# An attention-and-MLP kernel on one core: all products in 32-column shape, zero-padded queries for single score banks, and merges done by accumulating transfers

## The chip, the cores and the metric

The kernel runs on one core of a Trainium2 chip. The metric is the device time of one execution in microseconds (us); less is better. Engines are named as in the profile: PE is TensorE (PEld its weight loads), ACT is ScalarE, DVE is VectorE, POOL is GpSimd, and SP is SyncE, which here only issues transfers.

## The reference

For one sequence of 2048 rows and 448 columns, with 16 heads of 28 columns and a hidden width of 1792 (all data in bf16):

```python
xn = layernorm(A_x)
q, k, v = heads(xn @ A_wqkv)                       # 16 heads, 28 columns each
p = softmax(q @ k.T * 28 ** -0.5)                  # 2048 x 2048 scores for each head
s = merge_heads(p @ v) @ A_wo
g = silu(gelu(xn @ B_w1 + B_b1) @ B_w2 + B_b2)     # tanh form of GELU
out = A_x + s * g
```

`B_x` is not used. The exponentials are the large part: 16 x 2048 x 2048 of them.

## The kernel before

**Tiles.** Each head is padded to 32 rows, so that four heads (a group, G = 4 of them) fill the 128 partitions. Queries are cut into C = 4 chunks of 512 and keys into T = 16 tiles of 128. A block is one group with one query chunk; there are 16 blocks, each of 64 score banks (16 key tiles x 4 heads), 1024 in all. A score bank holds 128 keys x 512 queries in one of seven PSUM banks called `ring`; the eighth bank, `acc`, holds the attention output of the current block. The last block is cut into three parts by query, so that the end of the kernel can start early.

**Scores** (L1617) contract over 32 rows, so they use a strip of 32 rows of PE; four of them with different strips run at once. **Attention products** (L2052) put 32 output rows (28 values, one sum, padding) into one strip of 32 columns of PE; four of them run at once too. All other products use the full 128 x 128 array: query and key projections (L1042), value projections (L1390), the first MLP layer (L1468), the second (L1537), the output projection (L2140), and a product with zeros that only keeps PE busy (L1227). Some projections do the last 32-row pieces of their contraction together with scores (L1058, L1423, L1438). So PE changes between three shapes.

**Exponentials.** ACT takes two or three neighbouring score banks in one instruction (L1671) and writes bf16 tiles. Some banks ("late" ones, four at a time, the heads of one key tile) go to DVE instead: L1901 turns the score into the bits of a bf16 by a multiply and an add to uint16, and L1960 makes two shifted copies of the four banks (2048 values a row) by integer adds, so that the sum of the three approximates the exponential better. The three copies are multiplied by the values, the two shifted ones by values scaled by 0.6875 (`vs`, L1985), which takes 12 attention products a late group. A **merge** adds the two shifted copies first, which leaves 8 products. Before, POOL does it in four additions of 512 columns (L1973).

**The end of a block.** `acc` is copied to SBUF (L2111); its four rows of sums go to DRAM (L2117) and come back spread over 128 partitions (L2119), POOL raises them to the power -1 (L2121), they go out again (L2123) and come back repeated over the rows (L2126), and POOL multiplies (L2130). The output projection of a query chunk needs all four groups. Between GM = 582 and the next units, ACT changes its table and does all GELUs at once, partly straight out of PSUM (L1515).

**Order.** A scheduler runs at build time: generators (`p_scores`, `p_exps`, `p_pv`, `p_late`, `p_f1` and others) offer tasks with an estimated duration, and `run` picks for each engine the task that can start first, within `EPS`, by priority. A row of tuned constants per block (`BP`) steers it. On a change of PE's shape it adds `SWITCH` = 0.1 us, and `rate` prefers tasks of the shape that PE is in. What comes out is one fixed list per engine. Engines wait for each other by semaphores, and each works strictly through its own list. `p_solo` and `attach` place late scores: in strips of rows that a pair of scores leaves free, or alone.

Of the kernel before, what the change touches and what calls it, by code (L numbers as in the profile page):

```python
# [16 lines left out]
DH = 28  # L17
# [13 lines left out]
BPN = ('S4', 'QF', 'MG', 'GQ', 'GE', 'EPS', 'HP', 'JIT', 'RM', 'RG', 'WT', 'PV0', 'PVC', 'MP', 'ND4', 'LU', 'JOINT', 'LQ', 'JMAX', 'DQ', 'URG', 'SLACK', 'UR', 'QLEAD', 'QDIST', 'R3')  # L31
BP = (
# [17 lines left out]
)  # L50
NQ = (14, 15, 11, 13, 12, 16, 14, 5, 16, 15, 16, 16, 16, 16, 14, 16)
# [10 lines left out]
MG, GQ, GE = 1, 4.0, 12  # L62
GP, MP4, GL = 4.64, 1, 1.2
# [25 lines left out]
SEM, OWN = 0.07, 0.03  # L89
# [5 lines left out]
EA = 1  # L95
G3P = 0
# [15 lines left out]

class _Task:
    __slots__ = ("E", "fn", "reads", "writes", "dur", "lat", "rank", "w", "mode", "rows", "port")
# [5 lines left out]
    def __init__(self, E, fn, reads=(), writes=(), dur=0.1, lat=0.05, prio=5, w=1.0, mode="full", rows=(), port=False):  # L120
        self.E, self.fn, self.reads, self.writes = E, fn, list(reads), list(writes)
        self.dur, self.lat, self.rank, self.w = dur, lat, prio, w
        self.mode, self.rows, self.port = mode, set(rows), port
        if E == DVE:
            ov = min(OVERLAP, 0.4 * self.dur)
            self.dur, self.lat = self.dur - ov, self.lat + ov


class _Kernel:
# [55 lines left out]
    def start_of(self, t):  # L185
# [14 lines left out]
        for b in t.writes:  # L200
            mine = b.w is not None and b.w[0] is own
            if not (t.E == PE and mine):
                s = max(s, (b.tw or 0.0) + (OWN if mine else SEM))
            s = max(s, b.tr + SEM)
        return s

    def put(self, t, start=None):
# [3 lines left out]
        sem = self.evsem[t.E]  # L211
        self.evcnt[t.E] += 1
# [6 lines left out]
        self.prog[t.E].append(lambda eng, f=t.fn, s=sem: f(eng).then_inc(s, 1))  # L219
        h = (sem, self.evcnt[t.E])  # L220
# [276 lines left out]
    def alloc(self):  # L497
# [16 lines left out]
        self.P = sb("P", [128, NP, 512], bf)  # L514
        self.E_sb = sb("E_sb", [128, 2, 512], bf)
# [94 lines left out]
        self.b_dum = B()  # L610
        self.b_vs = [[B() for _ in range(NS)] for _ in range(2)]
# [27 lines left out]
        self.s_x0b, self.s_wqk1 = self.sem("s_x0b"), self.sem("s_wqk1")  # L639
        self.s_out = [self.sem("s_out%d" % q) for q in range(14)]  # L640
        self.s_w = {n: self.sem("s_" + n) for n in ("wqk", "wv", "w1", "w2", "wo", "b")}

    def schedule(self):
# [41 lines left out]
        K.a_left = {}  # L685
        K.h3_free = False
# [328 lines left out]
    def t_tr(self, c, pr, h, bank, tok, prio=5):  # L1015
# [11 lines left out]
        return _Task(PE, f, K.b_xn[c % 3][2 * h:2 * h + 2] + [K.b_id], [tok], 0.225, 0.17, prio)  # L1027
# [71 lines left out]
    def p_first(self):  # L1099
# [32 lines left out]
        def tr(pr, h):  # L1132
# [10 lines left out]
            return _Task(PE, f, K.b_xn[0][2 * h:2 * h + 2] + [K.b_id], [tok], 0.225, 0.17, 0)  # L1143
# [11 lines left out]
        def proj(which, h, k, bank, tok):  # L1155
# [8 lines left out]
            return _Task(PE, f, [K.b_wqk[which][0], K.b_pads, K.b_xnT[0][k] if h else K.b_x0h[k]], [tok], 0.218, 0.17, which)  # L1164
# [24 lines left out]
    def p_q0(self, h, bank, tok):  # L1189
# [5 lines left out]
                                               skip_group_check=True), [K.b_qsq[h], K.b_bsel], [tok], 0.11, 0.17, 0)  # L1195
# [7 lines left out]
    def p_warm(self, cond):  # L1203
# [4 lines left out]
        while cond():  # L1208
            yield _Task(PE, lambda eng: eng.matmul(bank[:, 0:256], K.ident[:, :], K.E_sb[:, 0, 0:256], start=True, stop=True),
                        [K.b_id, K.b_pads], [tok], 0.22, 0.1, 95)  # L1210
# [9 lines left out]
    def p_busy(self):  # L1220
# [3 lines left out]
        def f(eng):  # L1224
            ins = None
            for _ in range(3):
                ins = eng.matmul(K.acc[:, 0:128], K.zero[:, :], K.ident[:, :], start=False, stop=True,  # L1227
                                 skip_group_check=True)
# [9 lines left out]
    def p_norm(self, g0, g1, pr=1):  # L1238
        K = self
        bank, tok = yield ("bank", lambda: True, pr)  # L1240
# [9 lines left out]
        yield _Task(PE, f, K.b_wsq[g0:g1] + [K.b_pads], [tok], 0.15 * n + 0.1, 0.1, pr, 0.15)  # L1250
# [27 lines left out]
    def p_tr(self, c, pr):  # L1278
        K = self
        bank, tok = yield ("bank", lambda: K.ln_done >= 2 * (c + 1) and K.ready(K.b_xn[c % 3], 0.5), 1.5)  # L1280
# [49 lines left out]
    def p_q(self, g, c):  # L1330
# [21 lines left out]
        yield _Task(PE, lambda eng: eng.matmul(bank2, K.bsel[:, :], qs, start=True, stop=True),  # L1352
# [27 lines left out]
    def t_v(self, ts, h0, h1, bank, tok, ks=range(KT)):  # L1380
# [3 lines left out]
        def f(eng):  # L1384
            ins = None
            for i, t in enumerate(ts):
                off = i * nh * DH
                for kt in ks:
                    ap = bass.AP(tensor=K.wv, offset=kt * WS + h0 * DH, ap=[[KT * WS, 128], [1, nh * DH]])
                    ins = eng.matmul(bank[:, off:off + nh * DH], K.xnT[:, kt, t * 128:(t + 1) * 128], ap,  # L1390
                                     start=(kt == 0), stop=(kt > 0), skip_group_check=True)
# [71 lines left out]
    def t_f1(self, c, ft, bank, tok, k, prio=None):  # L1463
# [3 lines left out]
        def f(eng):  # L1467
            return eng.matmul(bank, K.w1[:, k, ft * 128:(ft + 1) * 128], K.xnT[:, k, c * 512:(c + 1) * 512],  # L1468
                              start=(k == 0), stop=(k > 0), skip_group_check=True)
# [19 lines left out]
    def p_gelu(self):  # L1489
# [4 lines left out]
        for q, pc in enumerate(PIECES):  # L1494
# [16 lines left out]
            for f in range(f0, f0 + n):  # L1511
# [4 lines left out]
                        wr, 0.4267 * n + (0.1 if pc else 0.06) + (1.3 if q == 0 else 0), 0.05, -1)  # L1516
# [4 lines left out]
        K.tE[ACT] += 1.3  # L1521
# [5 lines left out]
    def p_f2(self, c, t):  # L1527
# [5 lines left out]
        for q in range(7):  # L1533
            def f(eng, q=q):
                ins = None
                for ft in (2 * q, 2 * q + 1):
                    ins = eng.matmul(ps, hv[:, ft, t * 128:(t + 1) * 128], K.w2[:, ft, :],  # L1537
                                     start=(ft == 0), stop=(ft == FT - 1))
# [205 lines left out]
    def unit_of(self, b, n=1):  # L1744
# [21 lines left out]
    def p_late(self):  # L1766
        K = self
        yield ("until", lambda: K.late_on)
        K.spawn(K.p_room(), 0)
        K.spawn(K.p_solo(), 0, lambda: len(K.lq) > 0 and K.urgent(K.lq[0][0]))  # L1770
# [29 lines left out]
    def p_solo(self):  # L1800
        K = self
        while True:
# [3 lines left out]
            now = lambda: len(K.lq) > 0 and K.can(K.lq[0][0], K.now) and (K.in_gelu() or K.next_m >= MTOT or K.urgent(K.lq[0][0]))  # L1806
# [13 lines left out]
            for (m0, u, m), x in rs:  # L1820
                K.spawn(K.p_apass(u, m0, m - m0, *x), m0)

# [121 lines left out]
    def p_expq(self, m0, u):  # L1944
# [7 lines left out]
        for _ in range(2):  # L1952
            v = K.unit_of(b)
# [9 lines left out]
        if MG and K.next_m < 64 * (m0 // 64 + 1) - GE and K.tE[POOL] < K.now + GQ:  # L1963
            v, w = us[1:]
            for k in range(0, 4, MP4):
                if MP4 > 1:
                    W, X = K.pair(v, w)
                else:
                    W, X = K.part(v, k), K.part(w, k)
                    if len(W.shape) != len(X.shape):  # L1970
                        W, X = (x if len(x.shape) == 3 else x.rearrange("p (a b) -> p a b", b=128) for x in (W, X))
                bs = K.b_U[v][k:k + MP4], K.b_U[w][k:k + MP4]
# [271 lines left out]
```

## Time and profile before

| | |
|---|---|
| median of 3 runs | 426.02 us (424.85 to 426.95) |
| span of the profiled execution, first to last instruction | 425.0 us |
| PE busy, instructions | 403.8 us, 3705 products |
| ACT busy | 407.8 us, 435 instructions |
| DVE busy | 345.9 us, 588 instructions |
| POOL busy | 214.2 us, 214 instructions |
| exponentials on ACT (L1671) | 346 of two banks, 32 of three |
| exponentials on DVE (L1901) | 236 banks |
| merges on POOL (L1973) | 64 additions for 16 merges |

The profiled execution is given by its span alone; the median of the timed runs lies 1.0 us above it. Instructions of PE and ACT overlap their neighbours, so a length in the profile is longer than the step from one start to the next, and a busy share near 100% does not tell by itself which engine is the limit.

### The profile page before, as it was taken

The page shows a single profiled execution, that of the slowest core. Times are in us where ns is not written, and L with a number is a line of the kernel's source. Part 1 is how long each engine was busy: PE and PEld are TensorE (multiplying, and loading weights), DVE is VectorE, ACT ScalarE, POOL GpSimd, SP SyncE. Part 2 cuts the span into 40 slices and gives each one's busy share as a digit, 9 for nine tenths or more (in the row PEclk, how much of TensorE's full clock was granted, in tenths as well). Part 3 has the DMA queues.
Part 4 walks back from the last instruction along what each step waited for, and adds up shares of the span by engine and source line. Part 5 has one row for each costly group of instructions (what it writes and reads, how often), then busy time and mean ns, then how long its engine had stood idle before and what let it go on. Part 6 is the DMA issues. An engine that isn't in the chain of part 4 may idle for free.

```text
span 425.0 us, 9807 instructions
## 1 busy us (share of the span) xinstructions
PE 403.8 (95%) x3705; PEld 134.1 (32%) x3705; DVE 345.9 (81%) x588; ACT 407.8 (96%) x435; POOL 214.2 (50%) x214
## 2 busy tenths in 40 slices
PE   6999999999999999999999999999999999999985
PEld 4533222333222222222223442332222233223452
DVE  8969998579989998999975127679789968899865
ACT  6999999999999999999999999999999999999983
POOL 7590330784291405406374324677599678523720
PEclk9999999999999999999999999999999999999998
DMA  8702000010000000100230100001000010206232
GB/s 259 267 3 39 2 27 2 2 26 17 27 1 27 2 25 4 29 2 2 59 122 27 26 0 2 2 3 26 2 3 25 3 28 2 69 3 113 25 73 66
DMA packets 17721, 15.31 MB, mean 36 GB/s; under 512 B 8893, under 2 KB 14761, under 8 KB 17642
## 3 DMA queue, kind: packets, MB, share of 16 engines
q1 hardware_dynamic: 16810, 13.07, 11.3%
q0 software_dynamic: 576, 0.92, 1.7%
q8 instruction: 30, 0.49, 0.5%
q10 hardware_dynamic: 288, 0.69, 0.4%
q14 instruction: 17, 0.14, 0.1%
HBM read 12.60 MB, written 2.94 MB: 37 GB/s over the span
## 4 chain that ended last, share of the span: by engine, by line
PE 66%; DVE 14%; ACT 13%; issue 5%; POOL 1%; POOLq 0%; DVEq 0%; ACTq 0%
PE ring L1617 17%; PE acc L2052 15%; PE ring L1468 9%; PE ring L1537 9%; ACT P L1671 9%; PE ring L1042 5%; ACT h L1671 3%; DVE w L1901 3%; PE ring L2140 2%; PE ring L1438 2%; PE ring L1390 2%; DVE x_sb L1960 2%; PE ring L1058 2%; DVE h L1960 1%; DVE h L1450 1%
## 5 line engine op out<-in xcount | busy, mean ns | idle before, releaser
L1671 ACT ACTIVATE P<-ring 128x1024 bf16<-128x1024 f32 (+1 forms) x262 | 259.2, 1114 | 1.5 <-PE ring L1617 1.1
L1617 PE MATMUL ring<-qT,kT 32*128 32x512 bf16 (+2 forms) x1152 | 148.6, 359 | 6.3 <-ACT P L1671 1.7
L1671 ACT ACTIVATE h<-ring 128x1024 bf16<-128x1024 f32 (+1 forms) x82 | 86.0, 1139 | 2.0 <-PE ring L1617 1.8
L1617 PEld LDWEIGHTS ring<-qT,kT 32*128 32x128 bf16 x1152 | 40.1, 91 | 121.3 <-ACT P L1671 59.8
L2121 POOL TENSOR_TENSOR rc<-rs,mone 128x16 f32<-128x16 bf16 x15 | 46.6, 3104 | 21.5 <-DMA rs<-sums 21.4
L1537 PE MATMUL ring<-w,h 128*128 128x448 bf16 x224 | 55.0, 356 | 0.6 <-ACT xnT L1671 0.5
L1468 PE MATMUL ring<-xnT,w 128*128 128x512 bf16 x201 | 54.3, 382 | 0.8 <-DVE w L1901 0.6
L2052 PE MATMUL acc<-P,vaug 128*32 128x512 bf16 (+2 forms) x627 | 52.8, 354 | 0.0
L1901 DVE TENSOR_SCALAR x_sb<-ring 128x512 uint16<-128x512 f32 x64 | 42.8, 685 | 8.4 <-PE ring L1617 8.0
L1671 ACT ACTIVATE xnT<-ring 128x1024 bf16<-128x1024 f32 (+1 forms) x34 | 35.4, 1119 | 1.6 <-PE ring L1617 1.6
L1901 DVE TENSOR_SCALAR w<-ring 128x512 uint16<-128x512 f32 x52 | 34.4, 684 | 1.0 <-PE ring L1617 0.7
L1901 DVE TENSOR_SCALAR h<-ring 128x512 uint16<-128x512 f32 x40 | 27.0, 686 | 3.7 <-PE ring L1617 3.2
L2130 POOL TENSOR_TENSOR qT<-x_sb,E_sb 128x512 bf16<-128x512 f32 x15 | 18.1, 1209 | 22.8 <-DMA x_sb<-recs 22.6
L1345 POOL TENSOR_TENSOR qsq<-qT 128x512 bf16<-128x512 bf16 x12 | 12.7, 1071 | 32.7 <-DVE qT L1339 31.4
L1468 PEld LDWEIGHTS ring<-xnT,w 128*128 128x128 bf16 x201 | 16.5, 97 | 28.0 <-issue 9.4
L2052 PE MATMUL acc<-h,vaug 128*32 128x512 bf16 x213 | 24.7, 385 | 0.3 <-DVE w L1960 0.2
L1537 PEld LDWEIGHTS ring<-w,h 128*128 128x128 bf16 x224 | 16.1, 97 | 25.8 <-issue 15.5
L1339 DVE CAST qT<-ring 128x512 bf16<-128x512 f32 x15 | 10.3, 686 | 13.2 <-PE ring L1042 13.1
L1985 POOL TENSOR_SCALAR vs<-vaug 128x128 bf16<-128x128 bf16 x32 | 10.2, 320 | 21.0 <-PE acc L2052 10.7
L2052 PEld LDWEIGHTS acc<-P,vaug 128*32 128x32 bf16 x627 | 13.9, 95 | 16.7 <-issue 13.7
L2140 PE MATMUL ring<-wo,qT 128*128 128x448 bf16 x64 | 17.0, 386 | 2.3 <-POOL qT L2130 1.5
L1450 DVE TENSOR_SCALAR h<-ring,b1c 128x512 bf16<-128x512 f32 x23 | 17.0, 744 | 2.4 <-PE ring L1438 1.2
(232 smaller groups left out, 657.0 us busy)
## 6 DMA issues: line engine op xcount, KB each, us to landing
x_sb<-recs SPq DMA_DIRECT2D x60, 64.0 KB, 2.0
w<-in_B_w_dram SPq DMA_DIRECT2D x1, 1568.0 KB, 7.7
w<-in_B_w_dram SPq DMA_DIRECT2D x1, 1344.0 KB, 8.5
x_sb<-in_A_x_dram SPq DMA_DIRECT2D x2, 448.0 KB, 5.6
out_dram<-in_A_x_dram SPq DMA_DIRECT2D x2, 448.0 KB, 10.0
out_dram<-h POOLq DMA_DIRECT2D x4, 224.0 KB, 4.3
out_dram<-h SPq DMA_DIRECT2D x8, 112.0 KB, 1.7
h<-in_A_wqkv_dram SPq DMA_DIRECT2D x3, 168.0 KB, 5.2
```

Of the source, the lines that this page charges most:

```text
L1042: return eng.matmul(bank, w[:, k, g * 128:(g + 1) * 128], K.xnT[:, k, c * 512:(c + 1) * 512], start=(k == 0), stop=(k > 0), skip_group_che ...
L1450: yield _Task(DVE, lambda eng: eng.tensor_scalar(dst, bank, K.b1c[:, ft:ft + 1], None, op0=ALU.add), [tok, K.b_b1c], wr, 0.69, 0.0, 2)
L1468: return eng.matmul(bank, K.w1[:, k, ft * 128:(ft + 1) * 128], K.xnT[:, k, c * 512:(c + 1) * 512], start=(k == 0), stop=(k > 0), skip_grou ...
L1537: ins = eng.matmul(ps, hv[:, ft, t * 128:(t + 1) * 128], K.w2[:, ft, :], start=(ft == 0), stop=(ft == FT - 1))
L1617: return eng.matmul(dst, K.kT[32 * j:32 * j + 32, g, t * 128:(t + 1) * 128], K.qT[32 * j:32 * j + 32, g, c * 512 + q0:c * 512 + q0 + nq], ...
L1671: return eng.activation(reg[:, i0:i0 + n, :], src, ACTF.Exp, scale=SM_SCALE)
L1901: yield _Task(DVE, lambda eng: eng.tensor_scalar(K.part(u, k).bitcast(dt.uint16), K.like(u, bank), SM_SCALE * LOG2E * 128.0, (127.0 - EXP_ ...
L1960: yield _Task(DVE, lambda eng, W=W, T=T, i=i: eng.tensor_scalar(W.bitcast(u16), T.bitcast(u16), float(SH[i]), None, op0=ALU.add), bT, bW, ...
L2052: return eng.matmul(K.acc[32 * j:32 * j + 32, q0:q0 + nq], w, ap[:, col:col + nq] if len(ap.shape) == 2 else ap[:, col // 128:(col + nq) / ...
L2121: yield _Task(POOL, lambda eng: eng.tensor_tensor(K.rc[:, :], K.rs[:, :], K.mone[:, 0:1].to_broadcast([128, 16]), ALU.pow), [K.b_srs, K.b_ ...
L2130: yield _Task(POOL, lambda eng: eng.tensor_tensor(dst, K.rb, E, ALU.mult), [K.b_rb, tE], [K.b_onT[g][c]], 1.15, 0.05, 1, port=True)
L2140: ins = eng.matmul(ps, K.qT[:, g, c * 512 + t * 128:c * 512 + (t + 1) * 128], K.wo[:, g, :], start=(g == 0), stop=(g == G - 1))
```

## The change

Full-array products become four products of 32 columns each (`_mm`), which run beside each other in the four column strips. They are then of the same shape as the attention products, so that `mode` now knows mostly rows and columns; only transposes, the norm products and the start keep the full array. For each block the queries of the fourth head are copied into a buffer whose other rows are zero (`qpad`); a late score of that head can then be computed over all 128 rows, in column shape, in a bank of its own (`p_alone`). The merge becomes one transfer on POOL's queue from SBUF to SBUF which adds to its destination (512 KB, eight semaphores in turn); there are 41 of them. From the twelfth block on (`RV` = 11, blocks 11 to 14) the reciprocal of the sums is taken by DVE and not by POOL. The constants per block, the number of late groups that may be taken (`NQ`) and some estimated durations differ, and with them the order on every engine. Late banks are 244 instead of 236.

```diff
-NQ = (14, 15, 11, 13, 12, 16, 14, 5, 16, 15, 16, 16, 16, 16, 14, 16)
+NQ = (14, 6, 16, 11, 11, 16, 14, 3, 9, 15, 16, 16, 5, 13, 5, 12)
...
+TXI, TXL = 0.95, 5.0
+CN, CS, SR = 1, 3.0, 1
+PJ = 3
...
+RV = 11
...
+def _mm(eng, out, w, x, start, stop):
+    ins = None
+    for q in range(0, 128, 32):
+        ins = eng.matmul(out[q:q + 32, :], w[:, q:q + 32], x, tile_position=(0, q), start=start, stop=stop, skip_group_check=True)
+    return ins
...
-            s = max(s, b.tr + SEM)
+            s = max(s, b.tr + (SEMW if t.mode == "row" and t.E == PE else SEM))
...
         def f(eng):
-            return eng.matmul(bank, w[:, k, g * 128:(g + 1) * 128], K.xnT[:, k, c * 512:(c + 1) * 512],
-                              start=(k == 0), stop=(k > 0), skip_group_check=True)
+            return _mm(eng, bank, w[:, k, g * 128:(g + 1) * 128], K.xnT[:, k, c * 512:(c + 1) * 512], k == 0, k > 0)
...
-        ok = [u for u in K.free_u if not (b >= 2 * C and u in (3, 4, 5, 11, 12, 13))]
-        return min(ok, key=lambda u: max(max(t.tr, t.tw or 0.0) for t in K.b_U[u])) if len(ok) >= n else None
+        age = lambda u: max(max(t.tr, t.tw or 0.0) for t in K.b_U[u])
+        return min(ok, key=lambda u: (age(u) > K.now + 1.0, (u in (16, 17, 18)) == flat, age(u))) if len(ok) >= n else None
...
+    def p_pad(self):
+        yield _Task(POOL, lambda eng: eng.memset(K.qpad[:, :], 0.0), [], [K.b_pad], 1.1, 0.05, 2)
+        for b in range(NBLK - 1):
...
+            sl = slice(32 * PJ, 32 * PJ + 32)
+            K.dma(SP, lambda eng, sl=sl, g=g, c=c: eng.dma_start(K.qpad[sl, :], K.qT[sl, g, 512 * c:512 * c + 512]), K.s_pad,
+                  reads=[K.b_qT[g][c]], writes=[K.b_pad], land=max(K.now, K.b_pad.tr, K.b_pad.tw) + 2.2)
...
+    def p_alone(self):
...
+            yield _Task(PE, lambda eng, g=g, t=t, bank=bank: _mm(eng, bank, K.kT[:, g, 128 * t:128 * t + 128], K.qpad[:, :], True, True),
+                        [K.b_pad, K.b_kT[g][t // 4]], [tok], 0.218, 0.17, CS)
...
-        if MG and K.next_m < 64 * (m0 // 64 + 1) - GE and K.tE[POOL] < K.now + GQ:
+        if MG and not {16, 17, 18} & set(us[1:]) and K.next_m < 64 * (m0 // 64 + 1) - GE and K.tE[POOL] < K.now + GQ:
             v, w = us[1:]
-            for k in range(0, 4, MP4):
...
-                yield _Task(POOL, lambda eng, W=W, X=X: eng.tensor_tensor(W, W, X, ALU.add), bs[0] + bs[1], bs[0], GP * MP4 / 4, 0.05 if k + MP4 < 4 else GL, 2, port=True)
+            W, X = K.unit[v], K.unit[w]
+            yield _Task(POOL, lambda eng: eng.dma_start(W, X, accum_op=ALU.add), K.b_U[v] + K.b_U[w], K.b_U[v], TXI, TXL, 2, tx=True)
...
+        if b >= RV:
+            yield _Task(DVE, lambda eng: eng.reciprocal(K.rc[:, :], K.rs[:, :]), [K.b_srs], [K.b_rc], 0.2, 0.05, 1)
+        else:
+            yield _Task(POOL, lambda eng: eng.tensor_tensor(K.rc[:, :], K.rs[:, :], K.mone[:, 0:1].to_broadcast([128, 16]), ALU.pow),
```

The same replacement of one full product by `_mm` is made in the value projections, both MLP layers, the output projection, the norm of the last block, the query norm and the product that keeps PE busy.

More of the change, by code (lines that the diff above doesn't have):

```diff
@@ L110, in __init__ @@
         self.tr = 0.0
+def _mm(eng, out, w, x, start, stop):
[3 more added lines that the diff above has]
+    return ins
 class _Task:
-    __slots__ = ("E", "fn", "reads", "writes", "dur", "lat", "rank", "w", "mode", "rows", "port")
+    __slots__ = ("E", "fn", "reads", "writes", "dur", "lat", "rank", "w", "mode", "rows", "port", "tx")
     @property
@@ L118, in prio, with __init__ @@
         return self.rank() if callable(self.rank) else self.rank
-    def __init__(self, E, fn, reads=(), writes=(), dur=0.1, lat=0.05, prio=5, w=1.0, mode="full", rows=(), port=False):
+    def __init__(self, E, fn, reads=(), writes=(), dur=0.1, lat=0.05, prio=5, w=1.0, mode="col", rows=(), port=False, tx=False):
         self.E, self.fn, self.reads, self.writes = E, fn, list(reads), list(writes)
         self.dur, self.lat, self.rank, self.w = dur, lat, prio, w
-        self.mode, self.rows, self.port = mode, set(rows), port
+        self.mode, self.rows, self.port, self.tx = mode, set(rows), port, tx
         if E == DVE:
@@ L639, in alloc @@
         self.s_x0b, self.s_wqk1 = self.sem("s_x0b"), self.sem("s_wqk1")
+        self.s_tx, self.n_tx = [self.sem("s_tx%d" % q) for q in range(8)], 0
         self.s_out = [self.sem("s_out%d" % q) for q in range(14)]
@@ L1026, in f @@
             return ins
-        return _Task(PE, f, K.b_xn[c % 3][2 * h:2 * h + 2] + [K.b_id], [tok], 0.225, 0.17, prio)
+        return _Task(PE, f, K.b_xn[c % 3][2 * h:2 * h + 2] + [K.b_id], [tok], 0.225, 0.17, prio, mode="full")
     def t_trev(self, E, c, pr, bank, tok, prio=2):
@@ L1142, in f @@
                 return ins
-            return _Task(PE, f, K.b_xn[0][2 * h:2 * h + 2] + [K.b_id], [tok], 0.225, 0.17, 0)
+            return _Task(PE, f, K.b_xn[0][2 * h:2 * h + 2] + [K.b_id], [tok], 0.225, 0.17, 0, mode="full")
         def trev(pr, h):
@@ L1163, in f @@
                 return ins
-            return _Task(PE, f, [K.b_wqk[which][0], K.b_pads, K.b_xnT[0][k] if h else K.b_x0h[k]], [tok], 0.218, 0.17, which)
+            return _Task(PE, f, [K.b_wqk[which][0], K.b_pads, K.b_xnT[0][k] if h else K.b_x0h[k]], [tok], 0.218, 0.17, which, mode="full")
         def kproj(h):
@@ L1226, in f @@
             for _ in range(3):
-                ins = eng.matmul(K.acc[:, 0:128], K.zero[:, :], K.ident[:, :], start=False, stop=True,
-                                 skip_group_check=True)
+                ins = _mm(eng, K.acc[:, 0:128], K.zero[:, :], K.ident[:, :], False, True)
             return ins
@@ L1239, in p_norm @@
         K = self
-        bank, tok = yield ("bank", lambda: True, pr)
+        bank, tok = yield ("bank", lambda: True, pr, 1.0, "full")
         n = g1 - g0
@@ L1249, in f @@
             return ins
-        yield _Task(PE, f, K.b_wsq[g0:g1] + [K.b_pads], [tok], 0.15 * n + 0.1, 0.1, pr, 0.15)
+        yield _Task(PE, f, K.b_wsq[g0:g1] + [K.b_pads], [tok], 0.15 * n + 0.1, 0.1, pr, 0.15, mode="full")
         for b in K.b_hf[1]:
@@ L1279, in p_tr @@
         K = self
-        bank, tok = yield ("bank", lambda: K.ln_done >= 2 * (c + 1) and K.ready(K.b_xn[c % 3], 0.5), 1.5)
+        bank, tok = yield ("bank", lambda: K.ln_done >= 2 * (c + 1) and K.ready(K.b_xn[c % 3], 0.5), 1.5, 1.0, "full")
         for h in range(2):
@@ L1805, in p_solo @@
                 return
-            now = lambda: len(K.lq) > 0 and K.can(K.lq[0][0], K.now) and (K.in_gelu() or K.next_m >= MTOT or K.urgent(K.lq[0][0]))
+            wide = lambda: K.tE[PE] <= K.now + 0.3 and sum(K.free_at(i) + SEM <= K.now + JOINT for i in range(len(K.banks))) >= min(SR, len(K.lq[0][2]))
+            now = lambda: len(K.lq) > 0 and K.can(K.lq[0][0], K.now) and (K.in_gelu() or K.next_m >= MTOT or K.urgent(K.lq[0][0])) and (SR < 2 or wide())
             yield ("until", lambda: now() or not K.lq)
```

90 lines of the change are left out of this document (59 added, 31 removed), and 34 rows, old and new, of the table BP.

## The prediction

> **What bounds the kernel now.** I read first the busy times of the page, then ScalarE's (ACT's) timeline and waits, then the chain of waits for TensorE's (PE's) pace, then the last 20 us. The page:
>
> ```profile
> PE 403.8 (95%) x3705; PEld 134.1 (32%) x3705; DVE 345.9 (81%) x588; ACT 407.8 (96%) x435; POOL 214.2 (50%) x214
> ```
>
> Two engines are nearly full. Which one leads is seen in ACT's timeline (start, length):
>
> ```profile
> 99.52 1.13 ACT L1671 ACTIVATE P<-ring 128x1024 bf16<-128x1024 f32 x1
> 100.42 1.57 ACT L1671 ACTIVATE h<-ring 128x1536 bf16<-128x1536 f32 x1
> 101.75 1.16 ACT L1671 ACTIVATE P<-ring 128x1024 bf16<-128x1024 f32 x1
> ...
> 226.18 1.28 ACT L1515 ACT_TABLE_LOAD   x1
> 255.13 5.65 ACT L1671 ACTIVATE P<-ring 128x1024 bf16<-128x1024 f32 x6
> ...
> 413.05 1.45 ACT L1671 ACTIVATE xnT<-ring 128x1536 bf16<-128x1536 f32 x1 [1.58 <-PE ring L1617]
> 414.40 1.45 ACT L1671 ACTIVATE P<-ring 128x1536 bf16<-128x1536 f32 x1
> ```
>
> Exps overlap: the step from start to start counts. It is 0.90 us for two score banks (99.52 to 100.42) and 1.33 for three (to 101.75); over all undisturbed ones 0.904 and 1.331. From the first exp (12.77 in the same view) to the end of the last (415.85) are 403.1 us. Exps: 346 x 0.904 + 32 x 1.331 = 355.4. GELU with its table loads: 255.13 - 226.18 = 28.95. Four tanh: 3 x 1.59 + 1.21 = 6.0. So ACT waits 12.7 us in all, 3%. With 12.8 before and 9.2 behind, the span is 425.0. ACT sets the time wherever scores are ready.
>
> PE, from the chain of waits (start, length, what, how many):
>
> ```profile
> 109.87 0.55 PE acc L2052 x8
> 115.21 0.98 PE acc L2052 x16
> 247.64 3.45 PE ring L1468 x16
> ```
>
> A product 128 wide (L1468) takes 3.45 / 16 = 0.216 us for 512 columns. Eight 32-wide products (L2052), which run four at a time, take 0.55 and sixteen 0.98: 0.215 per four and 0.12 for the changes of shape around them. Start to start, a change of shape (32 rows, 32 columns, all 128) costs 0.10 beyond the columns, whichever two shapes they are (full to rows 312 ns, columns to rows 312, rows to full 317, rows to columns 315 for 512 columns of 213). The order holds 718 stretches of one shape. Streaming (columns / 2.4 GHz + 2.5 ns; the granted clock is 1.00 up to 388 us) is 304.4 us, the 717 changes 71.7: 376.1. What the starts show beyond that between 39 and 405 us is 24.5 us, PE's free time.
>
> **The change, part by part.** Counts are those of the two built programs.
>
> Exps. 367 instead of 378: 319 x 0.904 + 47 x 1.331 + one single at 0.48 = 351.4, against 355.4: **-4.0 us** on the engine that sets the time. The eight banks go to VectorE (DVE; L1901, 244 for 236, 0.685 each = +5.5) and bring two more pairs of shifted copies (L1960, 122 for 118 at 0.683 = +2.7).
>
> Merges. 16 merges were 64 additions on GpSimd (POOL, L1973, about 1.15 to 1.37 us each); 41 are now one issue each. The removed additions free POOL of 77 us, on which PE waited 0.2 us in all, and DVE of collisions: 17 of the 118 copies took far longer than 683 ns, 11.1 us in all, 4.1 of it beside L1973. DVE is 90 to 94% busy from 87 to 222 us, where ACT waits 5.6 us. I take **-1.0**, ends 0 and -4.1. The nearest rows for the new operation are the four accumulating stores at the end:
>
> ```profile
> L2166 POOL DMA_DIRECT2D out_dram<-h x4: 866/896/1411, 384.3 to 405.8; - x4
> ...
> DMA to landing us min/median/max: 4.1/4.3/5.5
> ```
>
> These move 224 KB each; the new ones 512 KB. The page's queue row (q0: 576 packets, 0.92 MB, 1.7% of 16 x 425 us = 116 us of engine time, 7.2 us over 16) gives 1.8 us of transfer in 4.3 us, so 2.5 around it. For 512 KB: 4.1 + 2.5 = 6.6 us (an estimate); the 448 KB plain loads (4.2 to 5.6) put the low end at 5, the slowest store (5.5) scaled the high end at 8. Who waits: PE, at the product that reads the merged unit, and behind it in PE's queue all scores. In emitted order 5 of the 41 have 6 exps between issue and that product (5.4 us), 2 have 7 (6.3), 7 have 8 (7.2), the rest 9 or more. At 6.6 us: 5 x 1.2 + 2 x 0.3 = 6.6 us of PE waiting, of which one exp already in the banks (0.9) covers nearly all: 5 x 0.3 = 1.5. I take **+0.7**, ends 0 and 10.1 (8.0 us: 5 x 1.7 + 2 x 0.8).
>
> Column shape. 804 products are cut into four. Longer column runs show 1.10 us for five steps of four, 0.220 against 0.216, so 804 x 4 ns = +3.2. Stretches fall from 718 to 683 (-3.5), streaming rises from 304.4 to 309.2, mostly the 35 padded scores (35 x 0.216 = 7.6, for shares of row groups that were nearly free). Sum 377.4 + 3.2 = 380.6: +4.5, so PE gets no relief. PE is free 24.5 us and ACT 12.7 in the middle; what falls into PE's free time costs nothing, so I let 12.7 / 37.2 of it through: **+1.5**, ends 0 and 4.5.
>
> By the Trainium skill (TensorEngine Tiling (Array Packing), "Available Configurations", "Restrictions") column tiling gives up the fast weight load, which speaks against the change. The row of L2052 disagrees: 0.215 per four with four loads each, hidden; by the rule the sum would be that of rival 4.
>
> Reciprocals. For the last four of the 15 blocks that take this path, the power on POOL (3.1 us) becomes a DVE reciprocal. It matters once, at the end:
>
> ```profile
> 410.93 1.14 POOL L2130 TENSOR_TENSOR qT<-x_sb,E_sb 128x512 bf16<-128x512 f32 x1 [4.26 <-DMA x_sb<-recs]
> 412.12 0.55 PE L2140 MATMUL ring<-wo,qT 128*128 128x448 bf16 x2 [1.54 <-POOL qT L2130]
> ```
>
> The projection waits for block 14's normalisation, scores queue behind it, and ACT loses the 1.58 us seen above. That chain runs from 395.3 to 412.1 with 3.3 us of power in it; 3 us less clears the wait: **-1.6**, ends -2.0 and 0. The reciprocal now waits on DVE for a transfer, with score evacuations (L1901) queued behind it, for whose banks PE waits. The scheduler allows 2 x 2.2 us for the two transfers ahead of it; block 14's took 5.04 (396.02 to 401.06): 4 x 0.64 = 2.6 at most, taken **+0.2**.
>
> Free: 14 small loads on SyncE of padded queries (32 x 512, 32 KB; the 64 KB loads land in 2.0) stand ahead of the normalisation's transfers, which have 20 us to spare except at the end; if not, a few tenths there. Start and padding's one fill: covered, POOL is 48% idle in 12.8 to 39 us. After the last exp, 11 projection products (L2140, 3.80 us in the chain) stand ahead of the last attention products now; in the new order 4 stand there, and 19 follow instead of 9: taken as nothing, ends -0.5 and +1.0.
>
> Sum: 425.0 - 4.0 - 1.0 + 0.7 + 1.5 - 1.6 + 0.2 = 420.8 of span. The median of the three runs, 426.02, is 1.0 above the profiled span: **421.8 us**.
>
> **The rivals.**
> 1. *Merges land late* (slower). The same five to seven products wait for their transfer. It decides from about 7.3 us from issue to landing, where 5 x 1.0 + 2 x 0.1 eats the gain; at 8.0 us it costs 10.1 instead of 0.7: 431. For it: the stores reached 5.5 us for 224 KB, and merges overlap in the second half. Against: packets here are larger and stay in SBUF. Chance 0.16. The Trainium skill (SBUF — State Buffer, "Who interferes with whom") says that DVE in a two-port mode locks POOL out of writing descriptors; the spread of 866 to 1411 ns agrees, and the copies run just there.
> 2. *PE becomes the bound.* All 4.5 us show and DVE's relief doesn't: 420.8 + 3.0 + 1.0 + 1.0 = 425.8, no change. For it: PE's free time is only 7%, and 5 us less time leaves 15 of 24.5. Against: of the weight loads' waits before scores 86.3 us (212 times, the change of shape in them) end with ACT, not with PE's own work. Chance 0.18.
> 3. *The new order closes ACT's waits.* Half of the 11 us that stay vanish: 416.3. For it: the stretches 109 to 222 us, where DVE is full, hold half of them. Against: 3% of waits is little to win from. Chance 0.12.
> 4. *Weight loads come out from cover* over long column runs. A load of 32 columns reads 95 ns in the groups; four in series less 216 ns is 164 ns x 804 = 132 us, so anything from 450 up. The trace has no column run above 40 products, so it can't be excluded: chance 0.02. It is what the rule on fast weight loads above would mean if loads were not hidden.
>
> That the stretches don't become fewer is no rival, the built order settles it.
>
> **How the numbers follow.** Forecast 0.52, rivals 0.16, 0.18, 0.12, 0.02. About 0.5%, 2.1 us, is what a measurement of this kernel can tell from none: faster is below 423.9, slower above 428.2. Of the forecast's 0.52, 0.44 lies below, 0.06 within; rival 2 gives 0.04 faster, 0.11 same, 0.03 slower; rival 3 0.12 faster; rival 1 and 4 slower but for 0.01. Faster 0.60, same 0.18, slower 0.22. The range takes in rivals 1 to 3 with most of their spread: 415 to 431. The forecast's own is 418 to 425.
>
> **What would show it.** Right: exps x367 at 0.904 and 1.331, waits of ACT below 13 us, none over 1 us in the last block; PE's column products at 0.22 per four; merges landing under 7 us and hardly any PE wait on them. Wrong: PE waiting for merge transfers by microseconds (rival 1), PE's free time near 15 us with ACT's waits up (rival 2), PE's loads ending its waits in long column runs (rival 4).

## The result and the profile after

| kernel | median | ratio to before |
|---|---|---|
| before | 425.44 us (424.74 to 426.95, 4 runs) | 1 |
| after | 452.5 us (449.81 to 454.85, 4 runs) | 1.0612, interval 1.0553 to 1.067 |

The change makes the kernel 6% slower, outside the predicted range of 415 to 431. In after's views L1634 are the scores, L1688 the exps, L120 the products of `_mm`, L2106 the attention products, L1962 the late banks on DVE, L2021 the shifted copies and L2027 the merges. The page's first lines and ACT's timeline (start, length, what; in brackets how long ACT had stood, and for whom):

```profile
span 448.9 us, 14450 instructions
...
PE 409.6 (91%) x6040; PEld 142.3 (32%) x6040; DVE 353.8 (79%) x604; ACT 407.1 (91%) x425; POOL 169.6 (38%) x188
...
PEclk9999599999999999999999999999999999999888
```

```profile
42.41 1.07 ACT L1688 ACTIVATE P<-ring 128x1024 bf16<-128x1024 f32 x1
50.33 1.02 ACT L1688 ACTIVATE P<-ring 128x1024 bf16<-128x1024 f32 x1 [6.85 <-PE ring L1634]
51.85 1.02 ACT L1688 ACTIVATE P<-ring 128x1024 bf16<-128x1024 f32 x1 [0.51 <-PE ring L1634]
...
417.58 1.99 ACT L1688 ACTIVATE xnT<-ring 128x1024 bf16<-128x1024 f32 x2
424.97 1.94 ACT L1688 ACTIVATE P<-ring 128x1024 bf16<-128x1024 f32 x2 [5.40 <-PE ring L1634]
429.45 6.52 ACT L1688 ACTIVATE P<-ring 128x1024 bf16<-128x1024 f32 x7 [2.54 <-PE ring L1634]
```

ACT's busy time is what it was (407.1 for 407.8), its share fell from 96% to 91%. Taken apart as in the prediction (the last column is an experiment told below):

| piece of the span, us | before | after | run 7 |
|---|---|---|---|
| up to the first exp | 12.8 | 13.7 | 13.6 |
| exps, undisturbed steps | 355.4 | 351.4 | 351.4 |
| GELU, table loads, tanh | 35.1 | 34.9 | 34.9 |
| ACT's waits between exps | 12.5 | 39.2 | 14.2 |
| behind the last exp | 9.2 | 9.7 | 11.1 |
| span | 425.0 | 448.9 | 425.2 |

The exps give back their 4.0 us; 26.7 us of waits come in. Two places hold 19.7 of the 39.2, block 0 (10.7) and block 15 (9.0); blocks 11 and 12 hold another 9.2.

**Block 0.** SP's timeline (issues, in SP's order) and then the chain of waits at the same place:

```profile
33.71 6.77 SPq L899 DMA_DIRECT2D wo<-in_A_wo_dram  x16
40.52 0.25 SPq L830 DMA_DIRECT2D w<-in_B_b_dram  x1
40.82 0.39 SPq L832 DMA_DIRECT2D b1h<-in_B_b_dram  x1
41.26 1.33 SPq L899 DMA_DIRECT2D out_dram<-in_A_x_dram  x2
42.63 0.59 SPq L1856 DMA_DIRECT2D qpad<-qT  x1
```

```profile
42.63 5.18 DMA qpad<-qT
...
47.85 1.04 PE ring L120 x8
```

The first padded query (L1856) stands in SP's queue behind the 16 loads of `wo`, two small loads and two copies of `x`: it is issued at 42.63, and lands 5.18 us later, beside what was issued ahead of it. PE stands for 5.87 us at the first padded score, with all other scores behind it. Its clock is halved meanwhile, from 43.4 us on, and stays so until 57.1. The windows (stretch; length; busy time and count of PE, PEld, DVE, ACT, POOL; granted clock, DMA share, GB/s):

```profile
48.00:52.00 4.00, 4.00 (x34) 0.80 (x30) 1.83 (x4) 1.17 (x2) 0.00 (x0) 0.50 0.00 0
52.00:56.00 4.00, 4.00 (x28) 0.58 (x20) 2.65 (x4) 2.92 (x3) 0.00 (x0) 0.50 0.00 0
56.00:60.00 4.00, 3.98 (x44) 0.91 (x42) 3.06 (x5) 3.39 (x4) 1.10 (x1) 0.87 0.00 0
...
417.00:423.00 6.00, 1.92 (x52) 1.12 (x48) 0.20 (x2) 2.57 (x3) 1.15 (x2) 0.94 1.07 182
423.00:427.00 4.00, 2.69 (x48) 1.62 (x52) 1.46 (x4) 1.94 (x2) 0.00 (x0) 0.50 0.39 74
```

At 0.50 two score banks take longer than ACT's step of 0.904, so ACT waits about 0.6 us before each exp up to 57 us. Blocks 0 and 1 together have 12.8 us of ACT's waits, where before had 1.4.

**Block 15.** The chain, with POOL's and DVE's timelines of the same time:

```profile
412.01 3.32 DMA sums<-E_sb
...
415.35 7.53 DMA rs<-sums
...
422.90 0.25 DVE rc L2176
```

```profile
410.11 1.35 POOL L2027 DMA_DIRECT2D wq<-xnT  x1 [2.89 <-DVE xnT L2021]
411.92 1.35 POOL L2027 DMA_DIRECT2D h<-h  x1 [0.46 <-issue]
413.72 0.85 POOL L2027 DMA_DIRECT2D xnT<-x_sb  x1 [0.45 <-issue]
```

```profile
422.90 0.25 DVE L2176 RECIPROCAL rc<-rs 128x16 f32<-128x16 bf16 x1 [5.80 <-DMA rs<-sums]
423.07 0.56 DVE L1581 SCALAR_TENSOR_TENSOR h<-w 128x448 bf16<-128x448 bf16 x1
423.55 0.61 DVE L2213 TENSOR_TENSOR h<-ring,h 128x448 bf16<-128x448 f32 x1
```

The sums of block 14, 4 KB each way, take 3.32 and 7.53 us while three merges of 512 KB are on their way, joined by a 224 KB store at 416.40 and a fourth merge at 416.94; the median of the second is 1.6. The 16 transfer engines read as full in 417 to 423 us (share 1.07 in the windows above). DVE stands at the reciprocal (L2176) for 5.80 us. Behind it in DVE's queue is L2213, which empties a bank of the output projection; the scores that need a bank wait for it, and ACT waits for them. The waits view (us in total, times, longest) names both places:

```profile
PE ring L120 <- DMA qpad<-qT: 10.7, 4, 5.9
...
DVE rc L2176 <- DMA rs<-sums: 6.0, 2, 5.8
...
PE ring L1634 <- DVE h L2213: 5.4, 1, 5.4
```

No PE row of this view names a merge. What the merges did is in the queue's row and in the padded queries' landings (issue to landing of `qpad`, 32 KB):

```profile
q0 software_dynamic: 6480, 22.42, 27.3%
```

```profile
DMA to landing us min/median/max: 1.8/3.5/5.2
```

### The profile page after: what moved, and what is told of

Its sections match the earlier page's. It is cut to its first block, busy times and chain, and to the rows that moved or that the text cites. A ratio compares the mean times of both kernels' runs of the same rounds, so it can differ in the third digit from the quotient of the medians.

```text
span 448.9 us, 14450 instructions
## 1 busy us (share of the span) xinstructions
PE 409.6 (91%) x6040; PEld 142.3 (32%) x6040; DVE 353.8 (79%) x604; ACT 407.1 (91%) x425; POOL 169.6 (38%) x188
## 4 chain that ended last, share of the span: by engine, by line
PE 47%; DVE 15%; ACT 14%; DMA 7%; issue 7%; POOL 2%; SPq 2%; DVEq 0%; ACTq 0%; POOLq 0%
PE ring L120 23%; PE ring L1634 11%; PE acc L2106 9%; ACT P L1688 8%; ACT h L1688 6%; DMA qpad<-qT 4%; DMA rs<-sums 2%; PE ring L1457 2%; DVE vaug L1962 2%; SPq L899 2%; DVE h L1962 1%; DVE x_sb L1962 1%; DVE kT L2021 1%; DVE h L2021 1%; DVE x_sb L2021 1%
## 5 line engine op out<-in xcount | busy, mean ns | idle before, releaser
L1688 ACT ACTIVATE P<-ring 128x1024 bf16<-128x1024 f32 (+1 forms) x251 | 258.9, 1130 | 24.8 <-PE ring L1634 24.1
L1634 PE MATMUL ring<-qT,kT 32*128 32x512 bf16 (+2 forms) x1117 | 145.4, 363 | 14.9 <-DVE h L2213 5.4
L1688 ACT ACTIVATE h<-ring 128x1024 bf16<-128x1024 f32 (+1 forms) x82 | 86.2, 1145 | 3.3 <-PE ring L1634 3.3
L1634 PEld LDWEIGHTS ring<-qT,kT 32*128 32x128 bf16 x1117 | 39.3, 92 | 132.5 <-ACT P L1688 52.8
L120 PE MATMUL ring<-w,h 128*32 128x448 bf16 x896 | 57.3, 359 | 0.0
L120 PE MATMUL ring<-xnT,w 128*32 128x512 bf16 x800 | 55.9, 382 | 0.1
L2106 PE MATMUL acc<-P,vaug 128*32 128x512 bf16 (+2 forms) x613 | 54.7, 362 | 0.4 <-DVE E_sb L2165 0.3
L1962 DVE TENSOR_SCALAR vaug<-ring 128x512 uint16<-128x512 f32 x68 | 45.5, 684 | 10.7 <-PE ring L1634 9.7
L1962 DVE TENSOR_SCALAR x_sb<-ring 128x512 uint16<-128x512 f32 x56 | 37.3, 684 | 4.9 <-PE ring L120 4.2
L2178 POOL TENSOR_TENSOR rc<-rs,mone 128x16 f32<-128x16 bf16 x11 | 35.4, 3219 | 9.2 <-DMA rs<-sums 9.2
L1688 ACT ACTIVATE xnT<-ring 128x1024 bf16<-128x1024 f32 (+2 forms) x34 | 32.7, 1035 | 1.2 <-PE ring L1634 1.1
L1962 DVE TENSOR_SCALAR w<-ring 128x512 uint16<-128x512 f32 x32 | 21.5, 686 | 12.7 <-PE ring L120 7.3
L1962 DVE TENSOR_SCALAR h<-ring 128x512 uint16<-128x512 f32 x40 | 26.6, 684 | 1.5 <-PE ring L1634 0.8
L2106 PE MATMUL acc<-h,vaug 128*32 128x512 bf16 (+1 forms) x216 | 27.6, 386 | 0.0
L120 PEld LDWEIGHTS ring<-xnT,w 128*32 128x32 bf16 x800 | 18.6, 96 | 25.5 <-issue 9.7
L120 PEld LDWEIGHTS ring<-w,h 128*32 128x32 bf16 x896 | 17.4, 95 | 24.0 <-issue 15.2
L120 PE MATMUL ring<-qpad,kT 128*32 128x512 bf16 x140 | 14.1, 398 | 11.5 <-DMA qpad<-qT 10.7
L1359 DVE CAST qT<-ring 128x512 bf16<-128x512 f32 x15 | 10.3, 689 | 17.5 <-PE ring L120 17.1
```

Of the source, the lines that this page charges most:

```text
L120: ins = eng.matmul(out[q:q + 32, :], w[:, q:q + 32], x, tile_position=(0, q), start=start, stop=stop, skip_group_check=True)
L1359: yield _Task(DVE, lambda eng: eng.tensor_copy(qb, bank), [tok], [qr], 0.7, 0.0, dp)
L1634: return eng.matmul(dst, K.kT[32 * j:32 * j + 32, g, t * 128:(t + 1) * 128], K.qT[32 * j:32 * j + 32, g, c * 512 + q0:c * 512 + q0 + nq], ...
L1688: return eng.activation(reg[:, i0:i0 + n, :], src, ACTF.Exp, scale=SM_SCALE)
L1962: yield _Task(DVE, lambda eng: eng.tensor_scalar(K.part(u, k).bitcast(dt.uint16), K.like(u, bank), SM_SCALE * LOG2E * 128.0, (127.0 - EXP_ ...
L2106: return eng.matmul(K.acc[32 * j:32 * j + 32, q0:q0 + nq], w, ap[:, col:col + nq] if len(ap.shape) == 2 else ap[:, col // 128:(col + nq) / ...
```

## The experiments

Theory A: two causes, the first padded query's place in SP's queue, and small transfers that are slow beside 512 KB merges. Rivals: DVE's reciprocal in itself, the column shape, the new order. Unless told otherwise the order on every engine is that of after. Waits are ACT's between exps, in the profiled run:

| run | 0 | 1 | 11 | 12 | 15 | other blocks | all |
|---|---|---|---|---|---|---|---|
| before | 0.9 | 0.5 | 0.2 | 0.8 | 2.5 | 7.6 | 12.5 |
| after | 10.7 | 2.1 | 5.3 | 3.9 | 9.0 | 8.2 | 39.2 |
| 1 loads later | 2.5 | 0.4 | 6.7 | 3.9 | 7.8 | 8.9 | 30.2 |
| 2 small merges | 10.8 | 2.1 | 1.6 | 3.9 | 0.8 | 7.3 | 26.5 |
| 5 both | 2.5 | 0.4 | 1.6 | 3.9 | 1.4 | 7.4 | 17.2 |
| 6 POOL copies | 2.6 | 0.4 | 0.8 | 2.6 | 9.2 | 7.2 | 22.8 |
| 7 and no last merges | 2.5 | 0.3 | 0.8 | 2.6 | 1.1 | 6.9 | 14.2 |

**Run 1, loads later.** In the generators of the `wo` loads and of the copies of `x`:

```diff
+            yield ("until", lambda: K.pad_b >= 1)
             K.wait(SP, K.b_wo.w)
```

> Compared with the changed kernel (452.5 us), only SyncE's order differs: the 16 loads of wo and the two copies of x to the output are issued behind the second padded-query load, not ahead of the first. Theory A (transfers come late: PE stands 5.9 us at 48 us for the first padded queries, whose load was issued at 42.6 behind those 18, and then runs at half clock to 56 us): the padded queries land at about 37 us, block 0's 10.7 us and block 1's 2.1 us of ACT waits fall to about 2 together, the time by 8 to 11 us to about 442. Rival B (column shape is slow on PE, or the order has too little room, so a wait removed comes back elsewhere): within 3 us of 452.

Measured 440.96 us, ratio 1.0355 (1.0304 to 1.0406): 11.5 us less than after, a little more than the 8 to 11 expected. Block 0's wait is 2.5, and the clock, in 40 slices of the span, no longer falls there (it still does for some 7 us each at block 11 and block 15, where the waits stay):

```profile
PEclk9999999999999999999999999999799999999799
```

**Run 2, small merges.**

```diff
-            yield _Task(POOL, lambda eng: eng.dma_start(W, X, accum_op=ALU.add), ...
+            yield _Task(POOL, lambda eng: eng.dma_start(W[:, 0:128], X[:, 0:128], accum_op=ALU.add), ...
```

> Same order on every engine as the changed kernel; the 41 merging transfers move 128 of their 2048 columns (32 KB instead of 512 KB), the rest of the merge is left out. Theory A says that the merges land in time but delay small transfers beside them: then the sums' trip of block 14 (3.3 + 7.5 us, alone 1.6 + 1.2) is short again, DVE's 5.8 us wait for it and the ACT waits of 5.6 and 2.7 us at 425 and 429 us go, and those of 1.3, 1.1 and 2.9 us for padded queries at 194, 313 and 323 us too: 12 to 14 us less, about 439. The first wait at 48 us stays (no merge is near it). Rival C (what delays is SyncE's queue order, not the merges): no more than 3 us less. Rival B: no change.

Measured 436.49 us, 1.0232 (1.0173 to 1.0292): 16.0 us less, more than the 12 to 14 expected, with block 0 as slow as in after. The padded queries land in

```profile
DMA to landing us min/median/max: 1.8/2.0/5.3
```

The median falls from 3.5 to 2.0; the longest, the first one, stays, and three others still take 3.1 to 4.3 us, so merges are not all that delays these loads. Of the merges it is the bytes that count, since their number and places are unchanged.

**Run 3, no wait for the sums in DVE's queue.** The reciprocal reads a column of ones (the normalisation of blocks 11 to 14 is left out):

```diff
-            yield _Task(DVE, lambda eng: eng.reciprocal(K.rc[:, :], K.rs[:, :]), ...
+            tk = _Task(DVE, lambda eng: eng.reciprocal(K.rc[:, :], K.ones[:, 0:1].to_broadcast([128, 16])), ...
+            tk.nowait = True
+            yield tk
```

> Same order on every engine; DVE's four reciprocals read a constant and so wait for no transfer (the normalisation of blocks 11 to 14 is left out). Theory A: the 5.8 us for which DVE stands still with score evacuations queued behind it go, and with them ACT's waits of 5.6 and 2.7 us in the last block: 6 to 9 us less, about 445; the others stay. If the last stall belongs to the late normalisation itself (the projection that waits for block 14) and not to DVE's queue, the wait only moves to that projection: under 3 us less.

Measured 450.58 us, 1.055 (1.0466 to 1.0633): 1.9 us less, within the spread of both kernels' runs, so the expectation of the theory missed. The other one, under 3 us, holds in its number, but not at the projection that it named. Block 15 still waits 6.8 us for 9.0, and in this execution blocks 0 and 11, which the edit doesn't touch, waited longer than in after's. The stall moved: PE now stands for a merge's own landing at an attention product.

```profile
PE acc L2107 <- DMA xnT<-x_sb: 2.7, 1, 2.7
```

So DVE's wait was not the cause but a symptom: that merge took 9.53 us to land and the one behind it 9.33, and with the transfers slow, the next one in line is late.

**Run 4, full shape.** `_mm` issues one product over the full array, in the order planned for columns:

```diff
...
-    for q in range(0, 128, 32):
-        ins = eng.matmul(out[q:q + 32, :], w[:, q:q + 32], x, tile_position=(0, q), ...
...
+    return eng.matmul(out, w, x, start=start, stop=stop, skip_group_check=True)
```

> Same order on every engine; each group of four 32-column products is one full product again. Changes of PE's shape rise from 682 to 753 (71 x 0.10 = +7 us of PE), streaming of 804 products falls by 4 ns each (-3 us). Theory A, for which column shape has nothing to do with the loss: within 4 us of the changed kernel, 450 to 456. Rival B: if column products, their weight loads or their many instructions are what is slow, 10 us or more less, below 443.

Measured 448.83 us, 1.0536 (1.048 to 1.0592): 3.7 us less, within the 4 us of theory A though below its 450, and the intervals of the two kernels overlap. The column shape isn't the loss. In the profiled executions blocks 0 and 1 have 9.4 us of waits for 12.8: PE stood for 4.7 us instead of 5.9, and the clock came back sooner, 0.68 in 48 to 52 us and 1.00 from there on. Runs 8 and 9 show no gain of that size.

**Run 5, both edits of 1 and 2.**

> The two edits of the first and second run together: the 16 loads of wo and the two copies of x stand behind the second padded-query load in SyncE's queue, and each merge moves 128 of 2048 columns (the rest of the merge's sum is left out). Theory A (the loss is two separate things: the first padded query held up on SyncE's queue, 11.5 us, and small transfers and late merges beside 512 KB transfers, 16.0 us): the savings add up, 452.5 - 27.5 = 425 us (422 to 428), ACT's waits 39.2 - 9.0 - 12.7 = 17.5 us. Rival B (both edits remove the same time, for example both ease the same transfers): 430 to 437 us.

Measured 427.84 us, 1.0041 (1.0016 to 1.0065), and waits of 17.2 us for the 17.5 expected. From after's 1.0612 run 1 took 2.57 points, run 2 3.80, both together 5.71: nine tenths of the sum (6.37), and the difference is no larger than what the intervals, half a point and more to each side, leave open. So there are two causes, they add up, and they hold nearly the whole loss.

**Run 6, loads later, full merges, and the padded query filled by POOL.**

```diff
-            K.dma(SP, lambda eng, ...: eng.dma_start(K.qpad[sl, :], K.qT[sl, g, 512 * c:512 * c + 512]), K.s_pad, ...
+            K.prog[POOL].append(lambda eng, ...: eng.tensor_copy(K.qpad[sl, :], K.qT[sl, g, 512 * c:512 * c + 512]) ...
```

> The 16 loads of wo later, as in the first run, merges full-sized, and the padded queries filled by a copy on GpSimd (32 rows x 512) instead of by a transfer. Theory A (small transfers slow beside the merges): no PE wait on a padded query above 1 us; ACT's wait of 6.7 us in block 11 falls to about 1.6 as with small merges, the wait of block 15 (7.8 us, sums and reciprocals beside merges) stays: 441.0 - 5 = 436 us (433 to 438). Rival C (what is slow in block 11 is the merged unit itself, and the padded query only ends last by little): 440 to 442 us.

Measured 435.35 us, 1.0221 (1.0137 to 1.0305). A copy takes 0.61 us (`L1862 POOL COPY`, 607 to 863 ns); the eight of 14 that ran while one or two merges were in flight took 607 or 608 ns. Block 11's wait falls from 6.7 to 0.8 and the rival falls with it. Block 15 keeps 9.2.

**Run 7, as run 6 and no merge in the last block.** The planner makes the last block anew, 37 merges instead of 41:

```diff
-    (2, 0, 1, 0.3, 11, ...
+    (2, 0, 0, 0.3, 11, ...
```

> As the run before, and no merges in the last block (37 instead of 41; the planner makes the last block anew, with the products of the unmerged units on PE; the order up to there is the same). It computes all of the reference. Theory A: block 14's sums and reciprocals land without a merge beside them, the 7.8 us of ACT's waits in block 15 fall to 1 to 2: 436 - 6.5 = 429.5 us (426 to 432), about 1% above the kernel before. Rival D (the products of four unmerged units keep PE as long as the transfers did): 434 to 437 us.

Measured 426.28 us, 1.0009 (0.9978 to 1.004). Block 14's way back of the sums, in run 6 and then in run 7 (the chain of run 6; issue to landing of `rs` from 390 us on in run 7):

```profile
394.81 3.53 DMA sums<-E_sb
398.36 7.46 DMA rs<-sums
```

```profile
DMA to landing us min/median/max: 1.6/1.6/1.6
```

Same instruction, same 4 KB, 7.46 us beside merges and 1.6 without. (The 224 KB store that runs beside this transfer in run 6 comes after it in run 7, and in run 2 too, where it takes 1.5 us, so the store's share isn't told from the merges'.) Block 15's wait falls from 9.2 to 1.1. This kernel computes all of the reference, keeps every part of the change, with 37 merges and the padded queries copied by POOL, and cannot be told from the kernel before.

**Run 8, the column shape alone,** put into the kernel before with its own order (each full product replaced by `_mm`).

> The kernel before with its own order, each full product (projections, MLP, values, selector, output projection) cut into four of 32 columns, nothing else changed: stretches of one shape 690 instead of 718, streaming 304.4 us by the same model, longest column run 500 products. The prediction's step (+4 ns per four, some 550 fours, less 28 changes of shape): between -1 and +2 us, 424.2 to 427.2 us. Rival E (the column shape costs what full products saved in the order of after, 3.7 us of 452.5): 428 to 430 us. Rival F (weight loads come out of cover): above 450 us.

Measured 427.08 us, 1.0027 (1.0004 to 1.0051): +1.2 us by the ratio, 0.2 to 2.2. Its first exp starts at 13.5 in the old order, and in runs 4 and 9, with full products in the new order, at 13.4 and 13.2; so what the 0.9 us at the start of after belong to stays open.

**Run 9, run 7 with full products again.**

> The mended kernel (loads of wo later, padded queries by GpSimd's copy, no merges in the last block), with every product that was cut into four as one full product again, in the same order of steps (749 stretches of one shape instead of 681, 3660 products instead of 6072); all of the reference. Theory A (the column shape costs about what the run on the order of before showed, 0 to 2 us, and more changes of shape give some of it back): 424.5 to 427 us, within 0.5% of the kernel before. Rival (full products gain the 3.7 us that they gained in the order of after): 422.5 us, faster than before by 0.9%.

Measured 426.7 us, 1.0006 (0.9981 to 1.0031), as run 7. Column shape or full shape is nearly the same here.

**Runs 10 and 11, run 7 with other settings for the last six blocks,** from two searches with the planner.

> The mended kernel with other settings for the last six blocks, found by letting the planner lay out the order some 1400 times and keeping the one that ends earliest by its own costs (1.07 us earlier, 39 merges); all of the reference. If the planner's costs hold now that loads, padded queries and the last merges are out of the way: 426.3 - 1.1 = 425.2 us. Rival (merges come beside block 14's sums and reciprocals again, since the planner knows nothing of slow small transfers): 430 us or more, with a transfer of sums or reciprocals over 5 us.

> As the run before, from another search (0.6 us earlier by the planner's costs, 37 merges): 425.7 us if its costs hold; 430 us or more if a merge comes beside block 14's sums and reciprocals.

Measured 426.86 us, 1.0018 (0.9988 to 1.0047), and 427.53 us, 1.0045 (1.0009 to 1.008). The gains that the planner counted don't show, and neither do the 430 us of the rivals: the longest way back of sums (`rs`) was 4.0 and 4.4 us. Single executions do reach 431 us, one of 12 and three of 12; the last section shows what happened in the first. No version here beats the kernel before.

## Why the prediction was wrong

Two steps failed. The merges were priced by the products that read them, and what they do to all other transfers was put at nothing (run 2: 16.0 us). The padded queries' loads were called free, and their place in SP's queue was not looked at (run 1: 11.5 us). The terms one by one:

**Exps, -4.0: right.** 319 of two banks at 0.90, 47 of three at 1.33, as taken.

**DVE's relief, -1.0: it did not come.** 13 of the 122 copies (L2021) still take over 0.8 us, 10.5 us beyond the usual 0.69; before it was 14 of 118 and 10.8 us. Taking the additions off POOL did not make the copies faster.

**Merges, +0.7: right in its own term, and the wrong term.** They land in 4.5, 5.2 and 9.2 us (least, median, most) where 6.6 was estimated, two of 41 later than that, and PE never waited for one in after. (The prediction gives no reason for taking 0.7 of the 1.5 us that its working gave.) What the sum did not hold is what 41 transfers of 512 KB do to other transfers: 16.0 us by run 2. Rival 1 had the right thing to watch, merges that overlap in the second half, but priced it at the merges' own readers (431 us).

**Column shape, +1.5: not contradicted.** Run 8 gives 1.2 us for the cutting alone. That the two numbers are close is in part luck: most of the prediction's 4.5 us were the padded scores, which run 8 doesn't have, and run 9, without any cutting, comes out as run 7. Fours follow at 0.22 us in the chain (two in 0.55, three in 0.76, the change of shape in them):

```profile
206.37 0.55 PE ring L120 x8
207.23 0.33 PE ring L120 x4
210.63 0.76 PE ring L120 x12
```

Rival 4 falls with it. Rival 2 doesn't account for the loss, but its 425.8 us lie beside run 7's 426.28, and whether PE is the limit there was not tested. The rule weighed in the prediction, that column tiling gives up the fast weight load (the Trainium skill, TensorEngine Tiling (Array Packing), "Restrictions"), costs nothing that run 8 shows beyond these 1.2 us.

**Reciprocals, -1.6 and +0.2: the sign was wrong beside merges.** The step "4 x 0.64 = 2.6 at most" took the slowest way of sums before (5.04 us for both transfers) as the worst case. It was 10.9 us (3.32 + 7.53), since before there was nothing of 512 KB beside it. A warning stood in the trace of before: block 14's way back of the sums took 3.4 us there instead of 1.6, beside one 224 KB store issued 0.8 us ahead of it, and these are the 5.04 us that the step counts with. Nor were score evacuations queued behind the reciprocal, but L2213, the multiply that empties the projection's banks. Run 3 shows 1.9 us, not clear of the spread, for the wait on DVE; with it taken away, the late merges stalled PE instead. Without merges in the last block (run 7) block 15 waits 1.1 us where before had 2.5, which is the -1.4 that the two terms add up to; that it comes from the reciprocal is not shown, since run 7 plans that block anew.

**"Free: 14 small loads on SyncE": a term put at nothing.** The prediction looked at what stands behind these loads (the normalisation's transfers) and not at what stands ahead of them. The view that shows it was there in the trace of before: SP's timeline has the 16 `wo` loads, 6.77 us of issuing, from 31.54 to 38.3 us, just where block 0's padded query has to go, and that query has a reader on PE within microseconds. It was taken at nothing; run 1 shows 11.5 us for the stand of 5.87 us and PE's half clock behind it. Nor did these loads land in the 2.0 us that the prediction quotes for 64 KB: their median was 3.5. The planner made the same mistake: it lands the load at `now + 2.2` whatever SP has ahead, and a transfer of sums at `lag` whatever runs beside it.

**Behind the last exp: within its ends** (+0.5 for -0.5 to +1.0).

**Where the -4.0 went once the two causes are gone** (run 7 against before, spans 425.2 and 425.0): +0.8 up to the first exp, +1.7 of waits (block 12 2.6 for 0.8, with PE behind DVE's evacuations, and block 0 2.5 for 0.9, against block 15 1.1 for 2.5), +1.9 behind the last exp, -0.2 of GELU. What lies behind the last exp may be the four unmerged groups' products; that is not shown, for run 9, with the same merges, has only 9.7 us there. What run 5 leaves of waits against before (17.2 to 12.5) is, by exclusion, the new order's: on balance it opens ACT's waits, so rival 3 was wrong too.

## What to carry to other kernels

A transfer that feeds a full engine is priced from the moment its queue is free, not from when its data are ready: read the issuing queue's timeline at that place, ahead of it first. A move of bulk work from an engine to DMA frees the engine and loads all other transfers: list the small ones with a reader close behind them, and keep the large ones out of their time, or make the small ones copies on an idle engine (0.61 us here, with merges in flight or without). A stand of PE costs its length and the half clock that may follow it.

## What the runs showed of the hardware

**PE's clock.** In all 13 profiles the record of the granted clock changes only on a grid of 3.41 us. In after it reads 0.50 from 43.41 to 57.07, from 323.31 to 326.72 and from 422.30 to 429.12 us: four steps of the grid, one and two. Leaving out the last 3 us of each span, it falls 15 times, each time at the end of a step in which PE stood once for 1.42 us or more: 1.44, 2.33 and 3.37 us inside the step in after, and 1.54 us even in before, at 410.6 us, for one step. The longest single stand inside a step that brought no fall is 1.27 us. A longer stand that lies across two steps need not: in run 8 PE stood for 1.81 us at 411.5 us, 1.00 of it in one step and 0.81 in the next, and the clock stayed. The Trainium skill (TensorE: Matmul & The Clock Gate, "What's actually happening") has the clock halved after an idle window of some 3.4 us. The length agrees with the grid; here less than half of it was enough.

So the price of a stall is more than its length. By run 1 the 5.87 us of block 0 were worth 9.9 us of ACT's waits (12.8 for 2.9 in blocks 0 and 1). In block 11 of after PE stood for a padded query for 2.33 us, and the clock was at 0.50 for the 3.41 us that followed. And the price depends on where a stand falls on the grid. In run 10's profile PE stood for 1.42 us at 164.0, all inside the step from 163.35 to 166.76; the clock was at 0.50 for the next three steps, and ACT lost 5.9 us in that block, where run 7 with the same order up to there lost 0.4 and PE did not stand:

```profile
165.00:170.00 5.00, 4.53 (x37) 0.94 (x37) 4.21 (x7) 2.84 (x4) 0.00 (x0) 0.68 0.24 43
170.00:175.00 5.00, 5.00 (x38) 0.89 (x35) 2.75 (x6) 3.43 (x4) 0.88 (x1) 0.50 0.30 58
```

That execution took 431.21 us, the longest of its kernel's. In run 9 PE stood for 1.22 us at the same place, inside one step, and the clock stayed at 1.00. How many steps the clock stays down is open: one behind 2.33 us in after, two and three behind the same stand in runs 1 and 3.

**Small transfers beside large ones.** Open is in what part of the transfer engines the small transfers wait beside the merges; run 2 shows that it goes with the merges' bytes, and in after the engines read as full where it was worst (share 1.07 in 417 to 423 us).
